# Windowed attention and a ReGLU FFN on one core: second and third half fed through the GpSimd queue and turned by TensorE, with a new order of the early work

## Chip, cores and metric

The kernel runs on one core of a Trainium2 chip. The metric is device time in microseconds (us) of one execution: the median of the runs, lower is better. In code and profile, PE is TensorE, PEld its weight loads, DVE VectorE, ACT ScalarE, POOL GpSimd, and SP SyncE, which only issues DMAs; SPq and POOLq are the engines' DMA issues.

## What is computed

Attention with a bias over 4 batches, 8 heads, 768 positions and 64 dimensions per head. A query sees 8 global keys and the 96 keys up to itself. Its output, as 3072 rows of 512, goes through a feed-forward network (FFN) with a relu gate.

```
scores = q @ k.T / 8 - slope[h] * dist       # dist: |i - j| for local keys, 96 for global ones
a      = softmax(where(global or local, scores, -1e9))
x      = (a @ v) as 3072 rows of 512
gate, val = relu(x @ w_gate), x @ w_val      # 512 x 1536 each
out    = (gate * val) @ w_out                # 1536 x 512
```

All inputs and the output are float32; the kernel computes with bf16 operands.

## The kernel before

The work is cut in eight halves `s`: batch `s // 2`, and in it the first or second 384 queries. Heads go in four pairs `p`. The keys of a batch lie in seven tiles of 128 rows, of which 8 are the global keys, repeated in each tile, and 120 are local ones.

For each half the attention needs q and k with the head dimension on the partitions. There are two ways to get there. The first two halves are loaded in float32, cast to bf16 (`piece_cast`, L238), transposed by TensorE with six 128x128 matmuls a pair (`piece_t`, L270), and copied out of PSUM by VectorE (`piece_copy`: L253 to L259 for the keys, L281 for the queries). From the third half on, `early_pieces` does it beside other work: GpSimd casts (L319, L327), six DMA transposes in SyncE's queue (L330, L334), and GpSimd puts the keys in order (L253 to L259 again).

Scores of a pair fill three PSUM banks. In the first half, and for pairs 0 and 3 of the second, the bias is added by matmuls with scaled identity matrices (`piece_bias`, L293), and q times k accumulates on it (`piece_biased`, L311, exp on ScalarE L316). Elsewhere exp comes first (`piece_qk`, L363, L366) and VectorE multiplies with a mask of exponentials (L375). Then come `piece_av_wide` and `piece_norm_wide` (L422, L432, L434, L437) in the first two halves, `piece_av` (L391 to L408) in later ones: sums and a times v on TensorE, the reciprocal as ln and exp on ScalarE, the product with it on VectorE, which writes `xT`.

The FFN of half `c` has 12 columns of 128. `gate(fc)` is four matmuls (L459) and a relu on ScalarE (L468); `val(fc)` is four matmuls and the product on VectorE (L475); `outp` multiplies with `w_out` (L482), ScalarE copies (L487), and SyncE stores (L488). The gate and value weights lie in three groups of four columns. All FFN results share three PSUM buffers.

The order on every engine is the order of the calls: `manual_schedule` keeps it, and an engine that waits holds up all that is behind it. What matters here:

- The first half is written out call by call. The second half's q and k are loaded in pairs by SyncE (`load_qk_after(1, True)`, after the first pair's attention), cast by GpSimd, and its attention is mixed by hand with the first half's FFN columns 0 to 5 (`F0`; `S1`, `TC1`, `AV1`).
- GpSimd issues the loads that cast: V (L121 for the eight global rows, L134 for a tile), weights (L151). Before the third half they come in the order V of batch 0 and weight group 0, V, group 1, casts of the second half, group 2, `w_out`, V of batch 1.
- After that GpSimd clears buffers (L632 to L636), writes the columns of ones in V's buffer (`fill_ones`, L139), loads the rest of V, and starts on the third half's casts. L634 clears the tile that the last of six small copies writes, in which SyncE spreads the global rows of V over the tiles (`spread_v_globals`, L126).
- `weave` takes a list of FFN items and puts other items into it at given shares of the list's nominal time, 0.65 for a gate or value item, 1.3 for half of an output item. The first weave has 20 items, columns of the two first halves, with the third half's `early_pieces` at 0.5 to 1.0. The second weave has 28 items, with the third half's attention at 0.2 to 0.92 and the fourth half's `early_pieces` at 0.1 to 0.6.
- Each later half's FFN is woven with the next half's attention and the early pieces of the one after it.

Of the kernel before, what the change touches and what calls it, by code (L numbers as in the profile page):

```python
# [8 lines left out]
FP32 = mybir.dt.float32  # L9
BF16 = mybir.dt.bfloat16  # L10
# [5 lines left out]
def kernel(  # L16
# [53 lines left out]
    rc_pool = ctx.enter_context(tc.tile_pool(name="rc", bufs=2))  # L70
    xt_pool = ctx.enter_context(tc.tile_pool(name="xt", bufs=3))
    ht_pool = ctx.enter_context(tc.tile_pool(name="ht", bufs=2))
    gr_pool = ctx.enter_context(tc.tile_pool(name="gr", bufs=3))
    osb_pool = ctx.enter_context(tc.tile_pool(name="osb", bufs=2))

    qk_psum = ctx.enter_context(tc.tile_pool(name="qkps", bufs=3, space=bass.MemoryType.PSUM))
# [25 lines left out]

    qs_of, ks_of = {}, {}

    def load_qk(s, h0, h1):
        b, half = divmod(s, 2)
        if s not in qs_of:
            qs_of[s] = stage.tile([128, H, NN * D], FP32, name="qs")
            ks_of[s] = stage.tile([128, H, NN * D], FP32, name="ks")
        for src, dst in ((k, ks_of[s]), (q, qs_of[s])):  # L110
            nc.sync.dma_start(
                out=dst[:, h0:h1, :],
                in_=src[b, h0:h1, half * QH : (half + 1) * QH, :].rearrange(
                    "h (p n) d -> p h (n d)", n=NN))

# [4 lines left out]
    def load_v_globals(b):  # L120
        nc.gpsimd.dma_start(out=v_dst(b, 0, NG, 0),  # L121
                            in_=v[b, :, 0:NG, :].rearrange("h p d -> p h d"))
# [5 lines left out]
    def copy_v_globals(eng, b, j0, j1):  # L128
        t = vbuf[b % 2][0:NG, :, D:].rearrange("p j (h z) -> p j h z", z=2 * D)[:, :, :, 0:D]
        eng.tensor_copy(t[:, j0:j1], t[:, 0:1].to_broadcast([NG, j1 - j0, H, D]))  # L130
# [22 lines left out]
    def load_w_group(i):  # L153
        load_w(wg[i], moe_w_gate, i * GW * 128, (i + 1) * GW * 128)
        load_w(wv[i], moe_w_val, i * GW * 128, (i + 1) * GW * 128)
# [11 lines left out]

    for p in range(HP):
        load_qk(0, 2 * p, 2 * p + 2)
    gsrc = setupp.tile([NG, 2, NN, WQ], FP32)  # L170
    gl = setupp.tile([NG, 2, NN, WQ], FP32)
    warm = setupp.tile([128, 128], BF16)
    nc.vector.memset(warm, 0.0)
    nc.vector.memset(ident, 0.0)
# [9 lines left out]
    for p in range(HP):  # L184
# [16 lines left out]
                            channel_multiplier=1)  # L201

    q1, q2 = [[1, NN], [NN, WQ]], [[0, 2], [-1, NN], [-NN, WQ]]
    nc.gpsimd.affine_select(out=gl[:, 0], in_=gsrc[:, 0], compare_op=ALU.is_ge, fill=BIG,
                            base=-NL, pattern=q1, channel_multiplier=-1)
    nc.gpsimd.affine_select(out=gl[:, 0], in_=gl[:, 0], compare_op=ALU.is_ge, fill=float(NL),
                            base=0, pattern=q1, channel_multiplier=-1)
    nc.gpsimd.affine_select(out=gl[:, 1], in_=gsrc[:, 1], compare_op=ALU.is_ge, fill=BIG,
                            base=-(NL - 1), pattern=q1, channel_multiplier=0)
    nc.gpsimd.affine_select(out=dd[0:NG], in_=gl, compare_op=ALU.is_ge, fill=BIG,  # L210
                            base=NL + KT - 2, pattern=q2, channel_multiplier=0)
# [4 lines left out]
    def setup_sid(h):  # L216
        nc.scalar.activation(sid[:, h], ident, AF.Copy, bias=0.0, scale=-slopes[h] / scale)
# [42 lines left out]

    tp_of = {}

    def piece_t(s, p):
        qk = cast_of[s, p]
        tp = av_psum.tile([128, 512], FP32, name="av_ps")
        tp = tp[:, 0:QH].bitcast(BF16).rearrange("d (i t) -> d i t", i=2)
        tp_of[s, p] = tp
        for i in (1, 0):
            for n in range(NN):
                nc.tensor.matmul(tp[:, i, n * 128 : (n + 1) * 128],  # L270
                                 lhsT=qk[:, i, n],
                                 rhs=ident, is_transpose=True,
                                 start=(i == 1 and n == 0), stop=(i == 0 and n == NN - 1))

    def piece_copy(s, p):
        b, half = divmod(s, 2)
        tp = tp_of[s, p]
        put_keys(nc.vector.tensor_copy, nc.vector.tensor_copy, kT[b % 2][p], tp[:, 1, :], half)
        for e in range(2):
            r = slice(64 * e, 64 * e + 64)  # L280
            nc.vector.tensor_copy(qTb[s % 2][r, p, e, :], tp[r, 0, :])  # L281
# [3 lines left out]
    def piece_bias(s, p):  # L285
        pool, name = (ff_psum, "ff_ps") if s == 0 and p % 2 else (qk_psum, "qk_ps")
        banks = [pool.tile([128, 512], FP32, name=name) for _ in range(3)]
        qk_of[s, p] = banks
        for g, bank in enumerate(banks_of_half[s % 2]):
            c = 0  # L290
            for i, (j, a, w, m) in enumerate(bank):
                for e in range(2):
                    nc.tensor.matmul(banks[g][:, c : c + NN * w], lhsT=sid[:, 2 * p + e],  # L293
                                     rhs=dd[:, 0 if j == 0 else 1, :, m : m + w],
                                     start=(i == 0 and e == 0), stop=False, skip_group_check=True)
                    c += NN * w

    def piece_biased(s, p):

        b, half = divmod(s, 2)  # L300
        kt = kT[b % 2][p]
        qd = qTb[s % 2][:, p].rearrange("d e (n p) -> d e n p", n=NN)
        es01 = es_pool.tile([128, 2, 480], BF16, name="es01")
        es2 = es_pool.tile([128, 480], BF16, name="es2")
        for g, bank in enumerate(banks_of_half[half]):
            ps = qk_of[s, p][g]
            es = es01[:, g] if g < 2 else es2
            c = 0
            for j, a, w, m in bank:
                n_ = 2 * NN * w  # L310
                nc.tensor.matmul(ps[:, c : c + n_], lhsT=kt[:, j, :], rhs=qd[:, :, :, a : a + w],  # L311
                                 start=False, stop=True, skip_group_check=True)
                for e in range(2):
                    es_of[s, p, j, e] = (es, c + e * NN * w)
                c += n_
            nc.scalar.activation(es[:, 0:c], ps[:, 0:c], AF.Exp, bias=0.0, scale=scale)  # L316
# [112 lines left out]
    def piece_norm_wide(s, p):  # L429
        av = av_of[s, p]  # L430
        ln = rc_pool.tile([128, QH], FP32, name="lnd")
        nc.scalar.activation(ln, av[0][:, 0:QH], AF.Ln, bias=0.0, scale=1.0)  # L432
        rc = rc_pool.tile([128, QH], FP32, name="rcp")
        nc.scalar.activation(rc, ln, AF.Exp, bias=0.0, scale=-1.0)  # L434
        if s not in xT_of:
            xT_of[s] = xt_pool.tile([128, N_DC, QH], BF16, name="xT")
        nc.vector.tensor_tensor(xT_of[s][:, p, :], av[1][:, 0:QH], rc, op=ALU.mult)  # L437
# [81 lines left out]
    def cast(s, p, ek, eq):  # L519
        piece_cast(s, p, 1, ek)  # L520
        piece_cast(s, p, 0, eq)
# [8 lines left out]

    for h in range(H):
        setup_sid(h)
    load_v_globals(0)
    for j in range(4):
        load_v(0, j)
    load_w_group(0)
    for h in (2, 3, 4, 5):
        setup_mask(h)
    warm_up(7)
    piece_bias(0, 0)  # L540
# [6 lines left out]
    piece_t(0, 1)  # L547
    piece_biased(0, 0)
    piece_copy(0, 1)
    piece_biased(0, 1)  # L550
    piece_bias(0, 2)
    piece_t(0, 2)
    piece_copy(0, 2)
    cast(0, 3, V, V)
    copy_v_globals(V, 0, 1, 4)
    piece_t(0, 3)
    piece_bias(0, 3)
    piece_biased(0, 2)
    piece_copy(0, 3)
    piece_av_wide(0, 0)  # L560
    piece_norm_wide(0, 0)
    load_qk_after(1, True)
    piece_biased(0, 3)
    piece_av_wide(0, 1)
    piece_norm_wide(0, 1)
    piece_av_wide(0, 2, qk_psum, "qk_ps")
    piece_norm_wide(0, 2)
    copy_v_globals(V, 0, 4, NT)
    for f in F0[0:3]:
        f(0, LAST)  # L570
    piece_av_wide(0, 3)
    piece_norm_wide(0, 3)

    zero_q(P, 1)
    for p in range(HP):
# [3 lines left out]
    for j in range(4, NT):  # L579
        load_v(0, j)  # L580
    load_w_group(1)
    for p in range(HP):
        cast(1, p, P, P)
    load_w_group(2)


    def S1(p):
        if p in (0, 3):
            piece_bias(1, p)
            piece_biased(1, p)  # L590
        else:
            for g in range(3):
                piece_qk(1, p, g)

    def TC1(p):
        piece_t(1, p)
        piece_copy(1, p)

    def AV1(p):
        piece_av_wide(1, p)  # L600
        piece_norm_wide(1, p)

    for f in F0[0:3]:
        f(LAST, N_DC)
    F0[3]()
    TC1(0)
    F0[4]()
    TC1(1)
    F0[5]()
    S1(0)  # L610
    F0[6]()
    TC1(2)
    F0[7]()
    TC1(3)
    S1(1)
    AV1(0)
    S1(2)
    AV1(1)
    F0[8]()
    S1(3)  # L620
    F0[9]()
    AV1(2)
    F0[10]()
    F0[11]()
    AV1(3)
    load_qk_after(2)
    for h in (0, 1, 6, 7):
        setup_mask(h)
    load_w(wo_sb, moe_w_out, 0, DM)
    load_v_half(2)  # L630
    for p in range(HP):
        nc.gpsimd.memset(kT[1][p][:, 3, 32:128].bitcast(mybir.dt.uint32), 0)  # L632
# [3 lines left out]
        nc.gpsimd.memset(qz[i].rearrange("t n p e z -> t (n p e z)").bitcast(mybir.dt.uint32), 0)  # L636
    for j in range(NT):
        fill_ones(nc.gpsimd, 1, j)
    load_qk(3, 0, H)
    load_v_half(3)  # L640
    weave(f1_1[G[0]] + f1_0[G[1]][4:] + f1_1[G[1]],
          [(0.1 + 0.1 * j, lambda j=j: fill_ones(nc.vector, 0, j)) for j in range(NT)],
          spread(early_pieces(2), 0.5, 1.0))
    weave(f1_0[G[2]] + f1_1[G[2]] + f2_0 + f2_1,
          spread(attention_pieces(2), 0.2, 0.92), spread(early_pieces(3), 0.1, 0.6))

    for c in range(2, NHALF):
        placed = []
# [43 lines left out]
```

The softmax here doesn't subtract the row's maximum and nothing guards it: scores larger than these inputs give would overflow.

## Time and profile before

| what | us |
|---|---|
| median of 8 runs | 275.51 |
| lowest, highest | 273.95, 276.91 |
| the profiled execution | 275.43 |
| its span, first to last instruction | 273.6 |
| TensorE busy | 241.9 |
| ScalarE busy | 157.1 |
| VectorE busy | 135.0 |
| GpSimd busy | 94.2 |
| HBM read, written (MB) | 28.38, 6.29 |

The span is about 2 shorter than the execution's time, in which start and end of the program lie too. Busy times are sums over the whole span, and engines work side by side. In 40 slices of the span, a digit gives the busy share in tenths. A timeline row has the start, the duration, the engine, the line and the operation, and in brackets the idle time before it and what ended it. A row of the waits has the total, the number, and the longest.

### The profile page before, as it was taken

The numbers are of one execution on the slowest core, as the hardware profiler recorded it, in microseconds if no ns is written. First come the engines' busy times: TensorE is split into PE (matmuls) and PEld (weight loads), VectorE is DVE, ScalarE is ACT, GpSimd is POOL, SyncE is SP. The second block draws the span as 40 slices with busy tenths as digits, with TensorE's granted clock in tenths as the row PEclk, the third lists the DMA queues.
The fourth block names the chain that finished last, engine by engine and source line by source line (L and its number), as shares of the span: only waits on it lengthen the run. The fifth ranks groups of instructions, "written<-read, shape, count | busy, mean of one in ns | idle before, by whom it ended". The sixth has DMA issues, their size and how long they took to land.

```text
span 273.6 us, 4719 instructions
## 1 busy us (share of the span) xinstructions
PE 241.9 (88%) x1658; PEld 142.5 (52%) x1667; DVE 135.0 (49%) x339; ACT 157.1 (57%) x323; POOL 94.2 (34%) x229
## 2 busy tenths in 40 slices
PE   7475788996069999999999999999999999999994
PEld 4353555563035555665566556655665566656641
DVE  5753484643025424674368537661767166623410
ACT  7572188432027656885677567865676578744321
POOL 8951770049573800652055424630343000000000
PEclk9999799999659999999999999999999999999999
DMA  6999499988544896567376098682853210021002
GB/s 194 151 183 248 116 186 200 258 236 89 123 92 95 143 122 189 152 150 84 99 230 146 11 191 241 141 72 85 261 89 86 77 41 0 2 78 38 2 38 77
DMA packets 82263, 34.31 MB, mean 125 GB/s; under 512 B 58176, under 2 KB 79168, under 8 KB 82240
## 3 DMA queue, kind: packets, MB, share of 16 engines
q1 hardware_dynamic: 50384, 26.11, 34.3%
q0 software_dynamic: 31856, 7.91, 29.5%
q8 instruction: 13, 0.21, 0.3%
q14 instruction: 10, 0.08, 0.1%
HBM read 28.38 MB, written 6.29 MB: 127 GB/s over the span
## 4 chain that ended last, share of the span: by engine, by line
PE 64%; issue 9%; DVE 6%; POOL 6%; DMA 6%; ACT 4%; SPq 3%; POOLq 0%; ACTq 0%
PE ff_ps L459 32%; PE ff_ps L482 22%; DMA ks<-in_k_dram 5%; PE av_ps L391 5%; PE qk_ps L363 4%; DVE xT L408 3%; POOL vbuf L134 2%; SPq L330 1%; ACT rcp L405 1%; ACT lnd L400 1%; DVE ht L475 1%; DMA qT<-qz 1%; POOL qk L238 1%; SPq L334 1%; DVE qk L238 1%
## 5 line engine op out<-in xcount | busy, mean ns | idle before, releaser
L459 PE MATMUL ff_ps<-xT,wg 128*128 128x384 bf16 x384 | 79.7, 328 | 4.2 <-DVE xT L437 2.9
L459 PE MATMUL ff_ps<-xT,wv 128*128 128x384 bf16 x384 | 79.8, 330 | 0.9 <-DVE ht L475 0.3
L468 ACT ACTIVATE grelu<-ff_ps 128x384 bf16<-128x384 f32 x96 | 46.8, 489 | 37.5 <-DVE ht L475 20.1
L475 DVE TENSOR_TENSOR ht<-ff_ps,grelu 128x384 bf16<-128x384 f32 x96 | 53.3, 555 | 27.7 <-PE ff_ps L459 19.4
L482 PE MATMUL ff_ps<-wo_sb,ht 128*128 128x512 bf16 x279 | 66.5, 379 | 0.4
L366 ACT ACTIVATE es<-qk_ps 128x432 bf16<-128x432 f32 (+2 forms) x78 | 40.8, 530 | 24.8 <-PE qk_ps L363 23.2
L375 DVE TENSOR_TENSOR es<-es,m_all 128x432 bf16<-128x432 bf16 (+5 forms) x118 | 36.2, 338 | 35.6 <-ACT es L366 35.1
L459 PEld LDWEIGHTS <-wv 128*128 128x128 bf16 x384 | 36.9, 99 | 27.7 <-issue 7.2
L408 DVE TENSOR_TENSOR xT<-av_ps,rcp 64x384 bf16<-64x384 f32 x48 | 26.7, 555 | 46.8 <-ACT rcp L405 42.2
L459 PEld LDWEIGHTS <-wg 128*128 128x128 bf16 x384 | 36.3, 98 | 24.4 <-issue 1.8
L482 PEld LDWEIGHTS <-ht 128*128 128x128 bf16 x288 | 26.8, 97 | 27.6
L363 PE MATMUL qk_ps<-qT,kT 128*128 128x432 bf16 (+5 forms) x118 | 26.7, 289 | 11.6 <-DMA qT<-qz 11.6
L319 POOL CAST kc<-ks 128x384 bf16<-128x384 f32 x24 | 12.1, 550 | 54.6 <-DMA ks<-in_k_dram 54.6
L400 ACT ACTIVATE lnd<-av_ps 64x384 f32<-64x384 f32 x48 | 23.3, 485 | 12.1 <-PE av_ps L391 11.3
L487 ACT COPY osb<-ff_ps 128x512 f32<-128x512 f32 x24 | 14.1, 585 | 23.7 <-PE ff_ps L482 22.8
L134 POOL DMA_DIRECT2D vbuf<-in_v_dram x28 | 24.5, 885 | 0.6 <-issue 0.3
L391 PEld LDWEIGHTS <-vbuf 128*128 128x128 bf16 x216 | 18.2, 98 | 8.2 <-issue 0.5
L363 PEld LDWEIGHTS <-kT 128*128 128x128 bf16 x118 | 11.4, 98 | 20.6 <-issue 12.9
L391 PE MATMUL av_ps<-es,vbuf 128*128 128x216 bf16 (+4 forms) x216 | 21.3, 226 | 0.3 <-DVE xT L408 0.2
L327 POOL CAST qz<-qs 128x192 bf16<-128x192 f32 x48 | 14.4, 349 | 1.4 <-DMA qs<-in_q_dram 1.2
L405 ACT ACTIVATE rcp<-lnd 128x384 f32<-128x384 f32 x24 | 12.5, 522 | 0.8
L316 ACT ACTIVATE es<-qk_ps 128x432 bf16<-128x432 f32 (+2 forms) x12 | 5.5, 531 | 9.1 <-PE qk_ps L311 9.1
(79 smaller groups left out, 137.3 us busy)
## 6 DMA issues: line engine op xcount, KB each, us to landing
out_dram<-osb SPq DMA_DIRECT2D x24, 256.0 KB
ks<-in_k_dram SPq DMA_DIRECT2D x6, 768.0 KB
qs<-in_q_dram SPq DMA_DIRECT2D x6, 768.0 KB
vbuf<-in_v_dram POOLq DMA_DIRECT2D x24, 120.0 KB, 5.1
ks<-in_k_dram SPq DMA_DIRECT2D x8, 192.0 KB
qs<-in_q_dram SPq DMA_DIRECT2D x8, 192.0 KB
wg<-in_moe_w_gate_dram POOLq DMA_DIRECT2D x3, 512.0 KB, 8.0
wv<-in_moe_w_val_dram POOLq DMA_DIRECT2D x3, 512.0 KB, 9.8
```

Source lines behind the costliest of these rows:

```text
L134: nc.gpsimd.dma_start(out=v_dst(b, NG + r0, NG + r0 + n, j), in_=v[b, :, KT * j + r0 : KT * j + r0 + n, :].rearrange("h p d -> p h d"))
L363: nc.tensor.matmul(ps[:, c : c + n_], lhsT=kt[:, j, :], rhs=qd[:, :, :, a : a + w], start=True, stop=True)
L366: nc.scalar.activation(es[:, 0:cols], ps[:, 0:cols], AF.Exp, bias=0.0, scale=scale)
L375: nc.vector.tensor_mul(e4, e4, mk)
L391: nc.tensor.matmul(av3[:, :, a : a + w], lhsT=vb[:, j, z0 : z0 + 128], rhs=es[:, c : c + NN * w].rearrange("k (n p) -> k n p", n=NN), star ...
L400: nc.scalar.activation(ln[o0 : o0 + 64], av[d0 : d0 + 64, 0:QH], AF.Ln, bias=0.0, scale=1.0)
L405: nc.scalar.activation(rc, ln, AF.Exp, bias=0.0, scale=-1.0)
L408: nc.vector.tensor_tensor(xT_of[s][r, p, :], av_of[s, p, e_][r, 0:QH], rc[r], op=ALU.mult)
L459: nc.tensor.matmul(st[key][:, 0:QH], lhsT=w_of(w, dc, fc), rhs=xT_of[c][:, dc, :], start=(dc == 0), stop=(dc == N_DC - 1))
L468: nc.scalar.activation(gr, psg[:, 0:QH], AF.Relu, bias=0.0, scale=1.0)
L475: nc.vector.tensor_tensor(ht[:, fc, :], psv[:, 0:QH], st["r", fc], op=ALU.mult)
L482: nc.tensor.matmul(ps2, lhsT=ht[:, fc, n * 128 : (n + 1) * 128], rhs=wo_sb[:, fc, :], start=(fc == 0), stop=(fc == N_FC - 1))
```

## The change

The loads. A new `load_qk_cast` has GpSimd load the second half's q and k with a cast to bf16 in the DMA, in two parts of four heads, between the loads of V and of weight group 0. The buffers are the old float32 ones, of which half is used. The third half's q and k are loaded uncast, but by GpSimd's queue too, behind weight group 2, and `w_out` comes right behind them. SyncE has no loads between the first half's and the six copies of V's global rows.

The transposes. The second half's are taken straight from the loaded bf16 buffer, one head at a time: twelve matmuls of 64 columns a pair. The third half is cast by GpSimd (`cast(2, p, P, P)`, pairs of casts as in the first halves), transposed by TensorE, and copied by VectorE; its four sets lie in the first weave at 0.6 to 0.9 of it, that is after 12, 14, 16 and 18 of its 20 items.

The order. The second half's attention follows directly on the first's, and the first weight group's products are in two parts: three gate columns between the second half's pairs 0 and 1, the fourth after its transposes, the four value columns between its later pairs. Pair 1 gets its bias by matmuls as well. There are four relu buffers, not three. In the first half some calls change places. The third half's attention lies at 0.02 to 0.8 of the second weave, not at 0.2 to 0.92. The distance tile of the global rows is bf16 and has a source of half the size.

```diff
-    gr_pool = ctx.enter_context(tc.tile_pool(name="gr", bufs=3))
+    gr_pool = ctx.enter_context(tc.tile_pool(name="gr", bufs=4))
...
+    def load_qk_cast(s, h0=0, h1=H):
+        b, half = divmod(s, 2)
+        for i, src, name in ((1, k, "ks"), (0, q, "qs")):
+            if (s, i) not in qk16:
+                t = stage.tile([128, H, NN * D], FP32, name=name)
+                qk16[s, i] = t.rearrange("p h x -> p (h x)").bitcast(BF16).rearrange(
+                    "p (h x) -> p h x", h=H)[:, :, 0 : NN * D]
+            nc.gpsimd.dma_start(
+                out=qk16[s, i][:, h0:h1],
                 in_=src[b, h0:h1, half * QH : (half + 1) * QH, :].rearrange(
                     "h (p n) d -> p h (n d)", n=NN))
...
-    gsrc = setupp.tile([NG, 2, NN, WQ], FP32)
-    gl = setupp.tile([NG, 2, NN, WQ], FP32)
+    gsrc = setupp.tile([NG, NN, WQ], BF16)
+    gl = setupp.tile([NG, 2, NN, WQ], BF16)
...
-    def piece_t(s, p):
-        qk = cast_of[s, p]
-        tp = av_psum.tile([128, 512], FP32, name="av_ps")
+    def piece_t(s, p, pool=av_psum, name="av_ps"):
+        tp = pool.tile([128, 512], FP32, name=name)
...
             for n in range(NN):
-                nc.tensor.matmul(tp[:, i, n * 128 : (n + 1) * 128],
-                                 lhsT=qk[:, i, n],
-                                 rhs=ident, is_transpose=True,
-                                 start=(i == 1 and n == 0), stop=(i == 0 and n == NN - 1))
+                for e in range(2 if s == 1 else 1):
+                    r = slice(64 * e, 64 * e + 64) if s == 1 else slice(0, 128)
+                    src = (qk16[s, i][:, 2 * p + e, n * D : (n + 1) * D] if s == 1
+                           else cast_of[s, p][:, i, n])
+                    nc.tensor.matmul(tp[r, i, n * 128 : (n + 1) * 128],
+                                     lhsT=src, rhs=ident, is_transpose=True,
+                                     start=(i == 1 and n == 0), stop=(i == 0 and n == NN - 1))
...
     load_v_globals(0)
     for j in range(4):
         load_v(0, j)
-    load_w_group(0)
+    load_qk_cast(1, 0, H // 2)
+    load_w(wg[0], moe_w_gate, 0, GW * 128)
+    load_qk_cast(1, H // 2, H)
+    load_w(wv[0], moe_w_val, 0, GW * 128)
...
-    load_qk_after(1, True)
     piece_biased(0, 3)
...
     for j in range(4, NT):
         load_v(0, j)
     load_w_group(1)
-    for p in range(HP):
-        cast(1, p, P, P)
     load_w_group(2)
+    load_qk(2, 0, H, nc.gpsimd)
+    load_w(wo_sb, moe_w_out, 0, DM)
...
+    piece_t(1, 0, *QKB)
+    AV(0, 2, *QKB)
+    piece_copy(1, 0)
+    piece_t(1, 1, *FFB)
+    AV(0, 3)
+    piece_copy(1, 1)
     S1(0)
-    F0[6]()
-    TC1(2)
-    F0[7]()
-    TC1(3)
+    gate, val = F0[0:8:2], F0[1:8:2]
+    gate[0]()
+    gate[1]()
+    gate[2]()
+    copy_v_globals(V, 0, 4, NT)
     S1(1)
-    AV1(0)
+    piece_t(1, 2)
+    piece_t(1, 3)
+    piece_copy(1, 2)
+    piece_copy(1, 3)
+    gate[3]()
     S1(2)
-    AV1(1)
+    val[0]()
+    val[1]()
+    AV(1, 0)
+    S1(3)
+    val[2]()
+    AV(1, 1)
+    val[3]()
+    AV(1, 2, *QKB)
     F0[8]()
-    S1(3)
+    AV(1, 3)
     F0[9]()
-    AV1(2)
     F0[10]()
     F0[11]()
-    AV1(3)
-    load_qk_after(2)
     for h in (0, 1, 6, 7):
         setup_mask(h)
-    load_w(wo_sb, moe_w_out, 0, DM)
     load_v_half(2)
...
-    load_qk(3, 0, H)
-    load_v_half(3)
+    for p in range(HP):
+        cast(2, p, P, P)
+    T2 = [(0.0, lambda p=p: TC(2, p, *QKB)) for p in range(HP)]
     weave(f1_1[G[0]] + f1_0[G[1]][4:] + f1_1[G[1]],
-          [(0.1 + 0.1 * j, lambda j=j: fill_ones(nc.vector, 0, j)) for j in range(NT)],
-          spread(early_pieces(2), 0.5, 1.0))
+          [(0.05 + 0.06 * j, lambda j=j: fill_ones(nc.vector, 0, j)) for j in range(NT)],
+          [(0.6, lambda: load_qk_after(3)), (0.6, lambda: load_v_half(3))],
+          spread(T2, 0.55, 0.95))
     weave(f1_0[G[2]] + f1_1[G[2]] + f2_0 + f2_1,
-          spread(attention_pieces(2), 0.2, 0.92), spread(early_pieces(3), 0.1, 0.6))
+          spread(attention_pieces(2), 0.02, 0.8), spread(early_pieces(3), 0.1, 0.6))
```

`QKB` and `FFB` name the PSUM pools of the scores and of the FFN. `AV(s, p)` is `piece_av_wide` and `piece_norm_wide`, and `TC(s, p)` is `piece_t` and `piece_copy`.

More of the change, by code (lines that the diff above doesn't have):

```diff
@@ L103, with load_qk @@
     qs_of, ks_of = {}, {}
-    def load_qk(s, h0, h1):
+    def load_qk(s, h0, h1, eng=nc.sync):
         b, half = divmod(s, 2)
@@ L110, in load_qk @@
         for src, dst in ((k, ks_of[s]), (q, qs_of[s])):
-            nc.sync.dma_start(
+            eng.dma_start(
                 out=dst[:, h0:h1, :],
+                in_=src[b, h0:h1, half * QH : (half + 1) * QH, :].rearrange(
+                    "h (p n) d -> p h (n d)", n=NN))
+    qk16 = {}
+    def load_qk_cast(s, h0=0, h1=H):
[7 more added lines that the diff above has]
+                out=qk16[s, i][:, h0:h1],
                 in_=src[b, h0:h1, half * QH : (half + 1) * QH, :].rearrange(
@@ L203 @@
     q1, q2 = [[1, NN], [NN, WQ]], [[0, 2], [-1, NN], [-NN, WQ]]
-    nc.gpsimd.affine_select(out=gl[:, 0], in_=gsrc[:, 0], compare_op=ALU.is_ge, fill=BIG,
+    nc.gpsimd.affine_select(out=gl[:, 0], in_=gsrc, compare_op=ALU.is_ge, fill=BIG,
                             base=-NL, pattern=q1, channel_multiplier=-1)
@@ L207 @@
                             base=0, pattern=q1, channel_multiplier=-1)
-    nc.gpsimd.affine_select(out=gl[:, 1], in_=gsrc[:, 1], compare_op=ALU.is_ge, fill=BIG,
+    nc.gpsimd.affine_select(out=gl[:, 1], in_=gsrc, compare_op=ALU.is_ge, fill=BIG,
                             base=-(NL - 1), pattern=q1, channel_multiplier=0)
@@ L532, with AV @@
         setup_sid(h)
+    QKB, FFB = (qk_psum, "qk_ps"), (ff_psum, "ff_ps")
+    def AV(s, p, *pool):
+        piece_av_wide(s, p, *pool)
+        piece_norm_wide(s, p)
     load_v_globals(0)
@@ L535 @@
         load_v(0, j)
-    load_w_group(0)
-    for h in (2, 3, 4, 5):
+    load_qk_cast(1, 0, H // 2)
+    load_w(wg[0], moe_w_gate, 0, GW * 128)
+    load_qk_cast(1, H // 2, H)
+    load_w(wv[0], moe_w_val, 0, GW * 128)
+    for h in range(2, 6):
         setup_mask(h)
@@ L549 @@
     piece_copy(0, 1)
+    piece_t(0, 2)
     piece_biased(0, 1)
-    piece_bias(0, 2)
-    piece_t(0, 2)
     piece_copy(0, 2)
@@ L555 @@
     copy_v_globals(V, 0, 1, 4)
+    piece_bias(0, 2)
+    piece_biased(0, 2)
     piece_t(0, 3)
+    piece_copy(0, 3)
     piece_bias(0, 3)
[L558 to L561, printed above, removed]
-    load_qk_after(1, True)
-    piece_biased(0, 3)
[L564 to L572, printed above, removed]
+    AV(0, 0)
+    piece_biased(0, 3)
+    AV(0, 1)
     zero_q(P, 1)
@@ L581, with TC @@
     load_w_group(1)
-    for p in range(HP):
-        cast(1, p, P, P)
     load_w_group(2)
+    load_qk(2, 0, H, nc.gpsimd)
+    load_w(wo_sb, moe_w_out, 0, DM)
     def S1(p):
-        if p in (0, 3):
+        if p == 2:
+            for g in range(3):
+                piece_qk(1, p, g)
+        else:
             piece_bias(1, p)
             piece_biased(1, p)
[L591 to L609, printed above, removed]
-    S1(0)
-    F0[6]()
-    TC1(2)
-    F0[7]()
-    TC1(3)
-    S1(1)
-    AV1(0)
-    S1(2)
-    AV1(1)
+    def TC(s, p, *pool):
+        piece_t(s, p, *pool)
+        piece_copy(s, p)
+    piece_t(1, 0, *QKB)
[4 more added lines that the diff above has]
+    piece_copy(1, 1)
+    S1(0)
+    gate, val = F0[0:8:2], F0[1:8:2]
[3 more added lines that the diff above has]
+    copy_v_globals(V, 0, 4, NT)
+    S1(1)
+    piece_t(1, 2)
[3 more added lines that the diff above has]
+    gate[3]()
+    S1(2)
+    val[0]()
[6 more added lines that the diff above has]
+    AV(1, 2, *QKB)
     F0[8]()
-    S1(3)
+    AV(1, 3)
     F0[9]()
-    AV1(2)
     F0[10]()
     F0[11]()
-    AV1(3)
-    load_qk_after(2)
     for h in (0, 1, 6, 7):
         setup_mask(h)
-    load_w(wo_sb, moe_w_out, 0, DM)
     load_v_half(2)
```

## The prediction

> **What bounds the kernel now.** I read the busy shares and the slices first, to see which engine is full and where it is not; times below are microseconds from the span's start, slices are 6.84 wide.
>
> ```profile
> PE 241.9 (88%) x1658; PEld 142.5 (52%) x1667; DVE 135.0 (49%) x339; ACT 157.1 (57%) x323; POOL 94.2 (34%) x229
> ...
> PE   7475788996069999999999999999999999999994
> ...
> PEclk9999799999659999999999999999999999999999
> ```
>
> TensorE (PE) is full from the thirteenth slice on. Its holes lie before 41 and in the tenth to twelfth slice (61.6 to 82). A hole costs only if TensorE has no slack later, and from 82 on it has none. So I ask what fills the late hole. The waits (us in total, times, longest):
>
> ```profile
> POOL vbuf L634 <- DMA vbuf<-vbuf: 18.9, 1, 18.9
> ...
> PE qk_ps L363 <- DMA qT<-qz: 11.6, 1, 11.6
> ```
>
> TensorE waits 11.6 once, for the third half's transposed q, whose makers are on GpSimd (POOL) and SyncE's queue. The timelines of these (start, duration):
>
> ```profile
> 58.38 0.55 POOL L634 MEMSET vbuf<- 128x544 uint32 x1 [18.93 <-DMA vbuf<-vbuf]
> 58.87 2.69 POOL L636 MEMSET qz<- 128x1536 uint32 x2
> 61.51 2.01 POOL L139 MEMSET vbuf<- 128x288 uint32 x7
> 63.67 2.45 POOL L134 DMA_DIRECT2D vbuf<-in_v_dram  x3
> 66.09 1.87 POOL L319 CAST kc<-ks 128x384 bf16<-128x384 f32 x4
> 67.89 2.38 POOL L327 CAST qz<-qs 128x192 bf16<-128x192 f32 x8
> ```
>
> ```profile
> 48.78 6.69 SPq L126 DMA_DIRECT2D vbuf<-vbuf  x6
> ...
> 67.99 3.92 SPq L330 DMA_TRANSPOSE kN<-kc  x3
> 72.02 3.94 SPq L334 DMA_TRANSPOSE qT<-qz  x3
> ```
>
> ```profile
> 65.22 0.81 PE L459 MATMUL ff_ps<-xT,wg 128*128 128x384 bf16 x4
> 77.60 0.52 PE L363 MATMUL qk_ps<-qT,kT 128*128 128x432 bf16 x1 [11.56 <-DMA qT<-qz]
> ```
>
> So one chain sets the end: batch 1's V globals land (48.8), SyncE copies them to six tiles (L126), GpSimd, stuck in order behind the last copy, wakes at 58.38, clears, casts, and six DMA transposes end at 77.5. After that 196.0 of TensorE-bound work remain to the end at 273.6. The V globals are late because the GpSimd queue serves them behind w_out (size, then us to landing, and the DMA rate in half-microseconds from 40 to 60):
>
> ```profile
> wo_sb<-in_moe_w_out_dram POOLq DMA_DIRECT2D x1, 1536.0 KB, 15.0
> ```
>
> ```profile
> GB/s 190 133 135 207 211 209 205 209 223 199 203 211 205 207 208 147 151 147 154 149 151 180 337 344 356 363 350 332 327 326 292 156 44 81 52 264 352 367 367 212
> ```
>
> w_out: issued 33.55, landed 48.5, at some 205 GB/s of destination bytes; then V at about 150; then float32 q/k at 330 to 367.
>
> **What the Trainium skill says.** "DMA: Bandwidth & Descriptors", section "SWDGE vs HWDGE vs iDMA": a DMA that casts must come from GpSimd, and only one software queue is allocated. The trace agrees: GpSimd's loads land in the order of issue (V tile 3 at 13.2, wg0 17.0, wv0 19.6, last V tile 21.4). The same page, "Specifications": below 512 bytes an element is read, modified and written. V's 128-byte rows run at 118 to 154 GB/s against 205 for the weights' 1 KB rows: it agrees in direction. "TensorE: Matmul & The Clock Gate", Part 1: idle TensorE falls to half clock and is released after some 3.4 us of work. Here 77.60 to 81.70 ran at a granted 0.55, as the windows show (clock is the third figure from the end):
>
> ```profile
> 77.60:81.70 4.10, 4.10 (x14) 1.91 (x15) 1.78 (x3) 1.55 (x3) 3.11 (x10) 0.55 0.30 68
> 81.70:104.10 22.40, 22.02 (x134) 11.84 (x135) 9.36 (x24) 14.32 (x29) 7.68 (x17) 1.00 0.71 122
> ```
>
> **Part 1, the second half (early work).** Removed: eight GpSimd casts (8 x 0.51), five VectorE mask multiplies of pair 1 (1.15). Added: one bias set (10 matmuls, 0.77), twice as many, half as wide transposes (48 for 24: between 0 and 4 x 0.34 more). Attention and first weight group change places. Before, the first weave (the FFN of the two first halves, woven together) starts at 45.89. TensorE idles about 6 between 20 and 46 and runs at a clock of 0.66 from 30 to 35, so the new order of both early halves can bring that start forward by 6 or more. I price this gain at nothing: in the new order TensorE meets the third half's first transpose after 12 of the first weave's items, 12 x 0.65 = 7.8 later, so at 53.7 at the latest, and has to wait there until 61.3 (part 3). That cover is 7.6; only if the early stage became slower by more than that would it cost.
>
> **Part 2, the one queue.** When do the V globals of batch 1 land now? I add up what the queue serves after V tile 3 (landed 13.2):
> - four casting half loads, 0.20 MB of bf16 each, 384-byte rows: not in this trace. At the weights' 205 GB/s 3.9 in all, at V's 118 6.7. I take 4.7 (167 GB/s, 1.18 each), as the row size lies between.
> - wg0 and wv0: 13.2 to 19.6, 6.4. The rest of V: 1.8.
> - four more weight loads at 205 GB/s: 4 x 2.56 = 10.2 (as high as 4 x 3.3 = 13.2, as wv2 took, 37.6 to 40.9).
> - third half's q and k, 1.57 MB uncast, at 350 GB/s: 4.5.
> - w_out 7.6 (40.9 to 48.5), globals 0.3.
> Sum: 13.2 + 4.7 + 6.4 + 1.8 + 10.2 + 4.5 + 7.6 + 0.3 = **48.7**; ends 47.3 and 53.9. Before it was 48.8: the queue takes 9.2 of q/k on, and gets back the gap from 28.8, where wv1 landed, to 32.08, where GpSimd issued the next load, and the slowing by the q/k loads beside it.
>
> **Part 3, the chain to the third half.** SyncE's queue now holds nothing ahead of the six copies (the third half's q/k had gone out at 47.44 and 47.90, and the first copy was stuck 3.06). Six issues 0.72 apart: the last starts at 48.7 + 0.1 + 3.6 = 52.4. It lands after 2.8 (a qT transpose: 74.65 to 77.46); 2.7 and 3.6 are the ends (first k load to its cast, 0.74 to 3.47; the last copy before, 54.80 to 58.38). So GpSimd wakes at 55.2, not 58.38. Memsets as before, 58.38 to 63.52: 5.1, to 60.3. The three V loads (2.45) now come behind the casts. First pair's two casts 0.96: **61.3**. Further pairs follow 0.96 apart, sooner than TensorE asks (1.64). DMA transposes and GpSimd's key copies of this half are gone.
>
> At 61.3 TensorE goes on. Before, it had done 29 FFN items when it got q at 77.60; now 12. The 17 missing cost 17 x 0.65 = 11.05. Four transpose sets come on TensorE: 0.34 each (34.45 to 34.79): 1.4. VectorE gets four copy sets of 1.4 beside one product of 0.56 per step, 1.96, where TensorE needs 1.30 + 0.34 = 1.64; 4 x 0.32 = 1.3, of which three FFN buffers and the slow clock at the start hide about half: 0.7 (ends 0 and 1.3). The clock penalty comes after the wait in both. State of 77.60 reached at 61.3 + 11.05 + 1.4 + 0.7 = 74.45. **Gain 3.15.**
>
> Edits at nothing: the third half's attention in 0.02 to 0.8 of the second weave, not 0.2 to 0.92 (TensorE idles there 0.4 in 22.4 now, which bounds it). Fourth half's loads behind SyncE's copies, at about 53, its casts and transposes on GpSimd and SyncE after 64 + 2.45: 4.3 of casts, 7.9 of transposes, done before 80, needed at about 101. The bf16 distance tile and a fourth relu buffer: early, covered.
>
> Sum: the profiled run took 275.43, of which the span is 273.6, and the median is 275.51, so the profile stands for it. 275.5 - 3.1 = **272.4**.
>
> **Rivals.**
> - Slower: the casting loads. If rows of 384 bytes cost a read and a write each, twice my 1.18, the queue runs 4.7 later, and each microsecond of it is one at the end: 275.5 - 3.1 + 4.7 = 277.1. It turns at 1.97 per half load. For: the 512-byte rule; against: V's smaller rows still made 118 GB/s.
> - No change: weight loads at 3.3 each, 3.0 later: 275.4. For: wv2; against: w_out's 205 GB/s.
> - Better: queue at its fast end (47.3) and VectorE hidden: 1.4 + 0.7 more, 270.3.
> - The wait goes: then TensorE runs on from 53.7 and the gain is 3.1 + 7.6 = 10.7, 264.8. It needs the globals landed by 41, with 7.6 of w_out ahead of them.
>
> **How the numbers follow.** Forecast (271 to 274.5) 0.50, better 0.15, no wait 0.05, no change 0.13, slower 0.17. 0.5%, 1.4, is about what a measurement of this kernel can tell from no change. Faster: 0.47 + 0.15 + 0.05 = 0.67; same 0.03 + 0.12 = 0.15; slower 0.18. The range, 269.3 to 277.2, holds forecast, no change, two thirds of better and a third of slower: 0.79.
>
> **What would show it.** Right: one TensorE wait of about 10 to 18 that ends near 61 with a transpose released by GpSimd's cast; GpSimd's memset released by a vbuf copy near 55; V globals landing near 48.7. Wrong: half loads over 1.9 each, the memset after 59, a gap later than 82 on TensorE, or no wait at the transposes.

## The result, and the profile after

The changed kernel takes 270.9 us (median of 11 runs, 269.65 to 271.44), against 275.61 (32 runs) of the kernel before on the same chips. The ratio is 0.9823, with a 95% interval of 0.9804 to 0.9842: 1.8% faster, where 272.4 (1.1%) was forecast. The profiled execution took 270.05 with a span of 268.0; it lies 0.85 under its median, so that the two profiled spans differ by 5.6, and the medians by 4.7. (Lines of code are shifted: L634 is now L653, L126 of the copies L141, `piece_t` L288.)

The page of the changed kernel, busy shares and slices of 6.70:

```profile
PE 240.6 (90%) x1717; PEld 143.0 (53%) x1725; DVE 137.0 (51%) x352; ACT 156.8 (59%) x323; POOL 90.3 (34%) x211
...
PE   7669996019999999999999999999999999999994
...
PEclk9999999658999999999999999999999999999999
```

From the fourth slice on the holes of the early stage are gone, and the late one has become one deep hole in the seventh to ninth slice (40 to 60). TensorE was busy for about as long as before (240.6 against 241.9); of the 5.6 by which the span is shorter, 4.3 are idle time. The waits name the same two steps as before, at their new lines (total, number, longest):

```profile
POOL vbuf L653 <- DMA vbuf<-vbuf: 16.1, 1, 16.1
...
PE qk_ps L288 <- POOL qk L253: 14.6, 1, 14.6
```

TensorE's wait has grown from 11.6 to 14.6, though the kernel is faster. The length of the wait alone does not tell what it costs: what counts is when it ends, and how much work TensorE still has then. The timelines of SyncE's queue, of GpSimd and of TensorE around it:

```profile
47.97 4.51 SPq L141 DMA_DIRECT2D vbuf<-vbuf  x6
52.66 0.38 SPq L111 DMA_DIRECT2D ks<-in_k_dram  x1
```

```profile
53.73 0.55 POOL L653 MEMSET vbuf<- 128x544 uint32 x1 [16.09 <-DMA vbuf<-vbuf]
54.22 2.69 POOL L655 MEMSET qz<- 128x1536 uint32 x2
56.86 2.01 POOL L154 MEMSET vbuf<- 128x288 uint32 x7
58.83 0.49 POOL L253 CAST qk<-ks 128x384 bf16<-128x384 f32 x1
59.28 0.49 POOL L253 CAST qk<-qs 128x384 bf16<-128x384 f32 x1
```

```profile
43.95 0.81 PE L476 MATMUL ff_ps<-xT,wv 128*128 128x384 bf16 x4
59.38 0.95 PE L288 MATMUL qk_ps<-ident,qk 128*128 128x128 bf16 x6 [14.62 <-POOL qk L253]
```

The chain is the predicted one: V's globals land (47.97), six copies follow without a stuck issue, GpSimd wakes at 53.73 and not at 58.38, clears, casts one k, and TensorE starts.

### The profile page after: what moved, and what is told of

Read it like the earlier page. It is cut to its first block, busy times and chain, and to the rows that moved or that the text cites. A ratio compares the mean times of both kernels' runs of the same rounds, so it can differ in the third digit from the quotient of the medians.

```text
span 268.0 us, 4798 instructions
## 1 busy us (share of the span) xinstructions
PE 240.6 (90%) x1717; PEld 143.0 (53%) x1725; DVE 137.0 (51%) x352; ACT 156.8 (59%) x323; POOL 90.3 (34%) x211
## 4 chain that ended last, share of the span: by engine, by line
PE 67%; POOL 9%; issue 8%; DMA 5%; DVE 5%; ACT 4%; POOLq 0%; ACTq 0%; DVEq 0%
PE ff_ps L476 36%; PE ff_ps L499 23%; DMA wv<-in_moe_w_val_dram 5%; PE av_ps L408 4%; PE qk_ps L380 4%; POOL vbuf L149 3%; DVE xT L425 2%; DVE ht L492 2%; ACT rcp L422 1%; ACT lnd L417 1%; ACT grelu L485 1%; POOL wg L166 1%; PE qk_ps L288 1%; POOL vbuf L154 1%; POOL ks L126 1%
## 5 line engine op out<-in xcount | busy, mean ns | idle before, releaser
L476 PE MATMUL ff_ps<-xT,wv 128*128 128x384 bf16 x384 | 78.3, 327 | 1.0 <-DVE ht L492 0.4
L476 PE MATMUL ff_ps<-xT,wg 128*128 128x384 bf16 x384 | 78.4, 328 | 0.3 <-DVE ht L492 0.2
L492 DVE TENSOR_TENSOR ht<-ff_ps,grelu 128x384 bf16<-128x384 f32 x96 | 53.1, 555 | 20.6 <-PE ff_ps L476 14.6
L476 PEld LDWEIGHTS <-wv 128*128 128x128 bf16 x384 | 36.3, 98 | 24.1 <-issue 3.1
L392 DVE TENSOR_TENSOR es<-es,m_all 128x432 bf16<-128x432 bf16 (+5 forms) x113 | 33.7, 327 | 26.4 <-ACT es L383 25.8
L383 ACT ACTIVATE es<-qk_ps 128x432 bf16<-128x432 f32 (+2 forms) x75 | 39.4, 529 | 10.1 <-PE qk_ps L380 8.1
L336 POOL CAST kc<-ks 128x384 bf16<-128x384 f32 x20 | 9.8, 536 | 58.3 <-DMA ks<-in_k_dram 58.3
L380 PE MATMUL qk_ps<-qT,kT 128*128 128x432 bf16 (+5 forms) x113 | 25.8, 286 | 0.3 <-DVE qT L298 0.3
L288 PE MATMUL qk_ps<-ident,qk 128*128 128x128 bf16 x24 | 2.4, 241 | 14.6 <-POOL qk L253 14.6
L344 POOL CAST qz<-qs 128x192 bf16<-128x192 f32 x40 | 11.9, 345 | 1.9 <-DMA qs<-in_q_dram 1.9
```

Of the source, the lines that this page charges most:

```text
L383: nc.scalar.activation(es[:, 0:cols], ps[:, 0:cols], AF.Exp, bias=0.0, scale=scale)
L392: nc.vector.tensor_mul(e4, e4, mk)
L476: nc.tensor.matmul(st[key][:, 0:QH], lhsT=w_of(w, dc, fc), rhs=xT_of[c][:, dc, :], start=(dc == 0), stop=(dc == N_DC - 1))
L492: nc.vector.tensor_tensor(ht[:, fc, :], psv[:, 0:QH], st["r", fc], op=ALU.mult)
```

## The experiments

Two theories stood against each other. Mine: the time is set by when GpSimd, held in order behind the last copy of V's global rows, casts the third half, and by how many FFN items TensorE has still to do then; the new early order is lost in the wait. The rivals gave the gain to the early order, or to TensorE's transposes. Each ratio below is to runs of the kernel before on the same chip; their medians were 276.12 for runs 1 to 4, 276.37 for runs 5 to 7, and 275.77 for run 8, so a difference between medians of different runs is good to a few tenths at best.

**1. The casts first.** In the changed kernel, GpSimd casts the third half ahead of its clearing.

```diff
     load_v_half(2)
+    for p in range(HP):
+        cast(2, p, P, P)
     for p in range(HP):
         nc.gpsimd.memset(kT[1][p][:, 3, 32:128].bitcast(mybir.dt.uint32), 0)
...
-    for p in range(HP):
-        cast(2, p, P, P)
     T2 = [(0.0, lambda p=p: TC(2, p, *QKB)) for p in range(HP)]
```

> GpSimd casts the third half's q and k before it clears buffers and writes V's columns of ones, not after; nothing else changes. My theory: TensorE's one late wait (14.6 us, ends at 59.4) is only GpSimd's place in its order behind the last copy of V's global rows; q and k had landed at 38 and 40. Then the first transpose follows at about 45 with no wait and no slow clock, V is ready at 59 where its first product comes at about 60, and the time is 270.9 - 14.3 - 1.4 = about 255. Rival 1, the copies' landing is needed a little later anyway: the wait moves to the first product with V and 8 or more of the 15.7 stay, 263. Rival 2, the wait comes from the q and k load itself: no change, 271.

Measured: **253.31**, ratio to before 0.9184 (0.9154 to 0.9215). GpSimd and TensorE in this run:

```profile
38.70 0.50 POOL L253 CAST qk<-ks 128x384 bf16<-128x384 f32 x1 [1.25 <-DMA ks<-in_k_dram]
40.84 0.51 POOL L253 CAST qk<-qs 128x384 bf16<-128x384 f32 x1 [1.63 <-DMA qs<-in_q_dram]
...
54.18 0.55 POOL L655 MEMSET vbuf<- 128x544 uint32 x1 [7.97 <-DMA vbuf<-vbuf]
...
57.32 2.02 POOL L154 MEMSET vbuf<- 128x288 uint32 x7
```

```profile
43.41 0.81 PE L476 MATMUL ff_ps<-xT,wv 128*128 128x384 bf16 x4
44.06 0.50 PE L288 MATMUL qk_ps<-ident,qk 128*128 128x128 bf16 x6
...
59.19 0.42 PE L408 MATMUL av_ps<-es,vbuf 128*128 128x216 bf16 x4
```

The transposes start with no idle time before them (no bracket), 15.3 sooner than in the changed kernel, and at full clock. The first product with V (59.19) comes just as V is complete: the last column of ones ends at 59.34, those of the tiles in use earlier. An earlier arrival would probably meet this as its next wait; no run here tests it. So moving one block of GpSimd's calls ahead of another gives 17.6 on top of the change. The profiled spans differ by 17.1: 15.3 is the earlier start, and 1.4 the slow clock that followed the wait and does not follow here.

**2. w_out behind V.** In the changed kernel, w_out's load comes behind `load_v_half(2)`.

```diff
-    load_w(wo_sb, moe_w_out, 0, DM)
...
     load_v_half(2)
+    load_w(wo_sb, moe_w_out, 0, DM)
```

> w_out's load is issued behind V of batch 1, not ahead of it. My theory (one queue, served in order): V's globals land 7.5 us sooner, at 40.4, the last copy at 46.3, the first transpose at 51.9, and the time falls by the same 7.5, to 263.4. Rival, the queue isn't what holds the globals (the landing is bound by the wait for an earlier load, or the copies by something else): less than 2 us of change, 269 to 271.

Measured: **267.01**, 0.9683 (0.9648 to 0.9717). The gain is 3.9, about half of the 7.5 expected. SyncE and GpSimd:

```profile
41.99 4.51 SPq L141 DMA_DIRECT2D vbuf<-vbuf  x6
```

```profile
51.06 0.55 POOL L653 MEMSET vbuf<- 128x544 uint32 x1 [13.90 <-DMA vbuf<-vbuf]
```

The globals landed 6.0 sooner (41.99 for 47.97), of the 7.5 expected. But from the first copy's issue to GpSimd's release it was 9.07, not 5.76: the last copy, issued near 45.8, took 5.2 to land instead of 1.9, with w_out now in flight beside it. Run 7 asks whether that is the cause.

**3. A slower early stage.** 30 idle matmuls ahead of the first weave of the changed kernel.

```diff
+    warm_up(30)
     weave(f1_1[G[0]] + f1_0[G[1]][4:] + f1_1[G[1]],
```

> 30 idle matmuls of 512 columns (about 6.4 us) are put on TensorE right ahead of the first weave: the early stage is made slower by that. My theory (the new order of the early work gains nothing, because its gain is lost in the later wait): no change, 270.9, and the wait for the cast shrinks from 14.6 to about 8. Rival, the early order is part of the gain: 277.3.

Measured: **270.48**, 0.9793 (0.9751 to 0.9835): no change, within the 1.2 either way that this interval leaves. TensorE:

```profile
36.66 6.64 PE L240 MATMUL ff_ps<-warm 128*128 128x512 bf16 x30
...
60.29 0.95 PE L288 MATMUL qk_ps<-ident,qk 128*128 128x128 bf16 x6 [9.20 <-POOL qk L253]
```

6.6 of useless work on TensorE cost nothing: the wait took it up. (The wait is 9.2, not 8, since GpSimd's release came 0.9 later in this execution.)

**4. The third half as before.** In the changed kernel, the third half goes back to `early_pieces(2)` at 0.5 to 1.0 of the first weave and its attention to 0.2 to 0.92 of the second; the queue and the early order stay.

```diff
-    for p in range(HP):
-        cast(2, p, P, P)
-    T2 = [(0.0, lambda p=p: TC(2, p, *QKB)) for p in range(HP)]
...
+    load_qk_after(3)
+    load_v_half(3)
...
+          spread(early_pieces(2), 0.5, 1.0))
```

> The change with the third half's transposes undone: GpSimd casts to the padded buffers, DMA transposes, GpSimd orders keys, attention at 0.2 to 0.92 of the second weave, as before; the loads in the one queue and the early order stay. My theory (the gain is that GpSimd wakes 4.7 us sooner, since nothing is ahead of the copies on SyncE; transposing on TensorE saves 13 us of chain but is asked for 17 items, 11 us, sooner and adds 1.4): transposed q at 72.8, 271.7, nearly as fast as the whole change. Rival, the transposes on TensorE are the gain: back to 275.6.

Measured: **272.03**, 0.9863 (0.9827 to 0.9899), within half a microsecond of the expectation. TensorE:

```profile
75.06 0.52 PE L380 MATMUL qk_ps<-qT,kT 128*128 128x432 bf16 x1 [19.14 <-DMA qT<-qz]
```

Transposed q was expected at 72.8 and came at 75.06. The profiled execution is the slowest of the four (273.14): in it the globals landed at 48.95, 1.0 later than in the changed kernel, and from the first copy's issue to GpSimd's release it was 7.1, not 5.8. Why the copies took longer here is open. By the medians, what run 4 takes back (TensorE's transposes and the earlier place in the weaves) is worth about 1 of the 4.7; the intervals overlap, so these runs do not tell it from nothing. The rival, 275.6, is out.

**5. Casts first, and the slower early stage.** The edits of 1 and 3 together.

> Both edits together: GpSimd's casts of the third half ahead of its clearing, and the 30 idle matmuls (6.6 us in the trace) ahead of the first weave. My theory: with the late wait gone the early stage is on the path, and what cost nothing in the changed kernel costs all of it here: 253.3 + 6.6 = 259.9. Rival, the early stage is covered by something else as well (the wait for V, say): 254 to 256.

Measured: **260.27**, 0.9417 (0.9391 to 0.9443). The same 30 matmuls cost 7.0 here by the medians (6.4 by the ratios), and nothing in run 3. The early stage is on the path once the wait is gone.

**6. The early stage as before, the third half cast first.** The kernel before, with the third half's loads, casts, transposes and places in the weaves of run 1.

```diff
     load_w_group(2)
+    load_qk(2, 0, H, nc.gpsimd)
+    load_w(wo_sb, moe_w_out, 0, DM)
...
-    load_qk_after(2)
...
     load_v_half(2)
+    for p in range(HP):
+        cast(2, p, P, P)
...
+    T2 = [(0.0, lambda p=p: (piece_t(2, p, qk_psum, "qk_ps"), piece_copy(2, p))) for p in range(HP)]
```

> The early stage as before (second half's q and k by SyncE, cast by GpSimd, old order of attention and first weight group), the third half as in the kernel that casts first (its q and k in GpSimd's queue behind weight group 2, casts ahead of the clearing, transposes by TensorE in the first weave). My theory: no late wait, first transpose at about 53.7 where the old order reaches it, so the new early order is worth the difference to 44.1, 9.6 us, once it is exposed: 253.3 + 9.6 = 262.9. Rival 1, the early order is worth little even then: 255. Rival 2, the order alone does nothing and the late wait comes back: 270 or more.

Measured: **264.82**, 0.9559 (0.9508 to 0.961); the interval is wide because one of the four executions took 261.72. TensorE:

```profile
54.43 0.50 PE L270 MATMUL qk_ps<-ident,qk 128*128 128x128 bf16 x6
```

The first transpose starts 10.4 after that of run 1, with no wait, and TensorE waits later twice, 1.30 and 0.51, for VectorE's products. So the new early stage is worth 11.5 by the medians (10.3 by the ratios) where it is exposed, and nothing that these runs can tell in the change as made. Run 6 puts back its loads, its order and its smaller edits together, so it does not say which of them gives how much.

**7. w_out behind the copies.** In the changed kernel, w_out's load is issued after GpSimd's release.

```diff
-    load_w(wo_sb, moe_w_out, 0, DM)
...
     nc.gpsimd.memset(vbuf[1][:, NT - 1, :].bitcast(mybir.dt.uint32), 0)
+    load_w(wo_sb, moe_w_out, 0, DM)
```

> The changed kernel with w_out's load issued after GpSimd has been released by the last copy of V's global rows, so that nothing large is in flight beside the copies. With w_out only behind V the globals landed 6 us sooner but the last copy 5.2 after its issue, not 1.9. Theory: the small copies were slowed by w_out's packets on the same DMA engines; without them the last copy lands near 47.7, the first transpose starts near 54.4, and the time is 267.0 - 2.3 = 264.7. Rival, the copies' landing has another cause: 267, or more by the 1 us that GpSimd needs to issue w_out.

Measured: **264.65**, 0.9575 (0.9547 to 0.9602). SyncE and GpSimd:

```profile
41.10 4.51 SPq L141 DMA_DIRECT2D vbuf<-vbuf  x6
```

```profile
46.87 0.55 POOL L652 MEMSET vbuf<- 128x544 uint32 x1 [11.95 <-DMA vbuf<-vbuf]
```

From the first issue to the release it is 5.77, as in the changed kernel, though the globals come as early as in run 2. With w_out not yet issued the copies are quick again, so w_out's load beside them was what slowed them in run 2. Of the release's 4.2 against run 2, 0.9 is the globals, which landed sooner in this execution, and about 1 is lost again to the issue of w_out that now follows.

**8. One call moved in the kernel before.** SyncE's loads of the third half's q and k come behind the six copies.

```diff
-    load_qk_after(2)
...
     load_v_half(2)
+    load_qk_after(2)
```

> The kernel before with one call moved: SyncE's loads of the third half's q and k come behind the six copies of V's global rows, not ahead of them. My theory (the change's gain is that nothing is ahead of the copies): globals land at 48.8 as before, the last copy 3.8 + 1.9 later at 54.5, not 58.4; the chain behind it is as before, and q and k, issued near 53, land by about 58, before GpSimd's cast asks for them near 62. The time falls by 3.9, to 271.7: most of the change's gain without its loads, order or transposes. Rival, the gain needs the loads in one queue (the copies are late for another reason, or the later q and k now hold the casts): 275 or more.

Measured: **272.04**, 0.9875 (0.984 to 0.991). SyncE, GpSimd, TensorE:

```profile
48.60 4.51 SPq L126 DMA_DIRECT2D vbuf<-vbuf  x6
```

```profile
54.37 0.55 POOL L634 MEMSET vbuf<- 128x544 uint32 x1 [15.09 <-DMA vbuf<-vbuf]
```

```profile
73.62 0.52 PE L363 MATMUL qk_ps<-qT,kT 128*128 128x432 bf16 x1 [9.49 <-DMA qT<-qz]
```

The copies take 4.51 to issue, not 6.69, GpSimd wakes at 54.37, and q comes 4.0 sooner (73.62 for 77.60). Moving one call takes 3.7 off 275.77 (2.5 to 4.4 by the interval), some three quarters of the 4.7 that the whole change gives.

## Why the prediction was right, point by point

**The mechanism** was right in each step. One wait of TensorE, released by GpSimd's cast, at 59.4 (predicted 61.3); GpSimd released by a copy at 53.7 (55.2); globals at 47.97 (48.7). Run 1 shows that this order on GpSimd, and nothing else, holds the third half; run 8 shows that clearing SyncE's queue ahead of the copies brings most of the gain.

**The early order at nothing** was right, and shown from both sides: run 3 (6.6 more, no cost) and run 5 (the same, 6.4 to 7.0). The cover was 14.6 and not the 7.6 of the prediction, since the new order brought TensorE to the transposes at about 44.8 and not at 53.7.

**The queue** was right within 0.7. The casting half loads, the item with no row in the trace before, I priced at 1.18 each, as the row size lies between those measured. In the changed kernel's DMA view (size, us from issue to landing), for the issues at 8.87, 9.64, 11.12 and 11.85:

```profile
ks<-in_k_dram POOLq DMA_DIRECT2D x1, 192.0 KB, 4.9
```

```profile
qs<-in_q_dram POOLq DMA_DIRECT2D x1, 192.0 KB, 5.2
```

```profile
ks<-in_k_dram POOLq DMA_DIRECT2D x1, 192.0 KB, 8.5
```

```profile
qs<-in_q_dram POOLq DMA_DIRECT2D x1, 192.0 KB, 8.9
```

They landed at 13.8, 14.8, 19.6 and 20.8, so the second of each pair took 1.0 and 1.2. The slower rival, a doubled price, fell. The other terms of the sum, read from the landings in the same way, hold too, the forecast in brackets: the half loads 4.2 in all (4.7), the first weight group 6.2 (6.4), the rest of V 2.0 (1.8), four more weight loads 10.6 (10.2), q and k 4.5 (4.5), w_out 7.5 (7.6); V tile 3, where the sum starts, landed at 12.8 (13.2). No term is off by more than 0.5. The 512-byte rule of the Trainium skill ("DMA: Bandwidth & Descriptors", "Specifications") is not visible as a step here: 0.197 MB in 1.0 to 1.2 is 164 to 197 GB/s for 384-byte rows, not far from the 205 of 1 KB rows.

**Where the size was off.** Forecast 3.15, in the profiles 5.6. The terms, in the prediction's order: the globals landed 0.8 sooner than before, where I had 0.1 (0.7 more). From the first copy's issue to GpSimd's release it was 5.8, against 9.6 before; I had 6.5, since I gave the last copy the 2.8 of a DMA transpose, and it took 1.9 (0.7 more). From the release to TensorE it was 5.65, and I had 6.1: TensorE transposes k first and needs only one cast (0.4 more). The slow clock after the wait cost 1.4, against 1.8 before, where I had the same in both (0.4 more). Together 2.2 of the 2.5; the rest is below what I can assign. The items TensorE had to make up, 17 x 0.65, and four transpose sets of 0.34 were as predicted. So was the hold by VectorE's copies, 0.7:

```profile
66.68 0.81 PE L476 MATMUL ff_ps<-xT,wv 128*128 128x384 bf16 x4
67.58 0.81 PE L476 MATMUL ff_ps<-xT,wg 128*128 128x384 bf16 x4
...
69.47 0.81 PE L476 MATMUL ff_ps<-xT,wg 128*128 128x384 bf16 x4 [0.24 <-DVE ht L492]
```

Items otherwise start 0.65 apart. The one at 67.58 is 0.25 late and the one at 69.47 is 0.4 late (one score matmul of 0.19 precedes it, at 68.88), each starting as VectorE's product ends (67.53, 69.42): 0.65 in all. The bracket shows less, because an item's bar of 0.81 reaches over the next start. That the medians differ by 0.9 less than the profiles is the spread of the runs, and no step.

**The slow clock.** The prediction took its cost as equal before and after. The windows of the changed kernel, clock third from the end:

```profile
59.38:62.43 3.05, 3.05 (x15) 1.68 (x15) 1.41 (x5) 0.49 (x1) 3.05 (x8) 0.54 0.00 0
```

One transpose set and two FFN items took 3.05 at a clock of 0.54 where run 1 needed 1.64 (44.06 to 45.70): 1.4 on top of the wait. Before, it was 4.10 at 0.55 (77.60 to 81.70): 0.45 of that, 1.8. Windows of 0.1 show half clock up to 62.1 and full clock from 62.2 after the change, and up to 81.2 and from 81.3 before. So the clock was released some 2.8 and 3.7 after TensorE went on, one under and one over the some 3.4 us of work that the Trainium skill states ("TensorE: Matmul & The Clock Gate", Part 1). The price of this step moved by 0.4 between two kernels.

**Of the rivals,** "the wait goes" did not come with the change, but run 1 made it true, and further than I had it (253.3, not 264.8), since I had set TensorE's arrival at the old order's 53.7. "Better" (270.3) came nearest to the measured time, but not by its reason: the globals landed at 47.97, not 47.3, and VectorE's copies were not hidden. What the prediction missed is the remedy. It held that the wait goes only if the globals land by 41; in run 1 they landed at 48.43, and the wait was gone, because GpSimd's casts had been written behind a wait that they do not need.

## What to carry to other kernels

On an engine that runs in order, look at what stands between a finished load and the work that needs it: here q and k had landed at 38 and 40, and their casts stood until 58.8 behind clearing that waited for something else. A stage that is made faster ahead of such a wait gains nothing until the wait is moved, and then nearly all of it at once (no cost of 6.6 of extra work in run 3, 10 to 12 between run 6 and run 1). And small copies that release others are best issued ahead of big loads in their queue: that alone gave 3.7 in run 8.

## What the runs showed of the hardware that was not expected

- The same six small copies within SBUF took, from first issue to release, 5.8 in the changed kernel and in runs 1, 3 and 5 to 8, 9.1 beside w_out's load in GpSimd's queue (run 2), and 9.6 behind 1.57 MB of loads in SyncE's own queue (the kernel before). In the last case one issue stood 3.06 instead of 0.7. Run 4, with 7.1, has no cause found.
- A pair's transposes as twelve matmuls of 64 columns, on alternate halves of the array, took no longer than six full ones. In the changed kernel's timeline a pair's two groups of six start at 15.85 and 16.02 and the next work at 16.19, so 0.34 in all; a full set of six took 0.34 too (64.06 to 64.40). The later two pairs, at 24.12 and 24.48, took 0.36 and 0.44 to the next start.
